# A new written order for all pieces of the first stage, and one layout for u's buffers

## The chip, the cores and the metric

The kernel runs on one core of a Trainium2 chip. The metric is device time in microseconds (us). The core has five engines, each with its own queue of instructions: TensorE (PE, with its weight loads as PEld), VectorE (DVE), ScalarE (ACT), GpSimd (POOL) and SyncE (SP), which issues the DMAs.

## The reference

The input `x` (2048 tokens, 512 channels, bf16) passes twice through a convolution layer A and an MLP layer B, each time as a residual:

```python
x = A_q
x = x + _A_ref(_layernorm(x), A_k, A_v, A_shift_k, A_ssm_k, A_ssm_D)
x = x + _B_ref(_layernorm(x), B_w1, B_b1, B_w2, B_b2)
x = x + _A_ref(_layernorm(x), A_k, A_v, A_shift_k, A_ssm_k, A_ssm_D)
x = x + _B_ref(_layernorm(x), B_w1, B_b1, B_w2, B_b2)
```

`_A_ref(q, k, v, ...)` shifts `k` by a four-tap filter for each channel, multiplies with `v` to u, convolves u along the 2048 tokens with `ssm_k` (a Fourier transform of length 4096, a product, a transform back), adds u times `ssm_D`, and multiplies with `q`. `_B_ref` is layer normalisation, a matmul to 1376 columns, gelu, and a matmul back to 512. k, v and the filters are the same in both A layers, so the convolution is computed once.

## The kernel before

The kernel has two stages. The first computes the convolution Y and the head of the first MLP; it runs to about 100 us. The second is a loop over eight groups of four token blocks (four groups, twice), each with two matmuls, `mm1` (L732) and `mm2` (L766), gelu on ACT and the normalisations on DVE.

The first stage is cut into some 340 pieces. A class `_Plan` collects them, each with a name and the code that it issues; `plan.write(ORDER)` then issues them in the order of a long string. A word of it is a name, a dot, the engine (P, A, D, G for POOL, S for SP) and digits for the buffers: a piece on PE names its slot of PSUM (`ps`, four of them) and, where it opens one, its buffer `xb` or `zt`. Each engine runs its own pieces strictly in this order, so a piece that waits holds all that stand behind it on its engine. A name with `e` at the end is the evacuation of the PE piece of that name, from PSUM to SBUF, on ACT or DVE (helper `evac`, L210 and L212), which frees the slot. The letters, with cc the quarter of the channels (0 to 3) and j the quarter of the 32 first-step frequencies:

- `lk`, `lv`, `lK`, `lW`, `lM`, `lx`, `w1`, `w2` and so on: loads. `kT`, `dg`, `kv`, `kvm`: the taps on PE and the product with v, for three quarters of the channels. `kg`, `ka`, `kgm`: taps, sums and the product with v of the last quarter, on POOL (L445, L452, L456), from which U3 starts.
- `KS`, `K2`: both steps of the filter's transform; `sa`, `sb`: eight copies of its result to a second layout (512 KB each).
- `U{cc}S{q}`: first step of u's transform, 4 matmuls into one PSUM slot, evacuated to a buffer `ZT` (L302). `U{cc}T{h}`: its 128x128 blocks transposed, 16 on PE for the quarters 0 to 2 (L334, evacuated at 128x2048), by DMA for quarter 3 (L281).
- `X{cc}{j}`: second step (L548), evacuated to an `xb` buffer. `T{cc}{j}`: the product of that buffer with the filter's spectrum, in SBUF, 128x2048 elements, on DVE or POOL (L563). T33 is cut into halves a and b. `V{cc}{j}`: first step of the transform back (L571), evacuated into a `ZT` buffer, or into the arena for quarter 0.
- `Z{cc}{g}`: transposes of V's results by DMA (L619) for the quarters 0 to 2, and `TD{g}` on PE (L607) for quarter 3; g is the token group. `Y{g}{t}`: last step (L639).
- `s00` to `s02`, `g`, `h`, `p`, `b`: normalisation, gate, statistics, power (POOL, L248) and normalisation again of the first token group; `LT`: its transposes (L647); `M`: the first MLP matmul (L695), which needs `w1`. Its gelu is L703.

The product of a T piece reads an `xb` buffer twice and two blocks of the spectrum, which it overwrites:

```python
kk = at(64 * K + 8 * K * cc + 2 * ka * CW, [[-32 * K, 2], [1, n * CW]])
x2 = apf(xb, xb.offset + (ka - k0) * CW, [list(xb.ap[0]), [0, 2], [1, n * CW]])
eng.tensor_tensor(kk, x2, kk, ALU.mult)
```

`w1` is loaded over the filter's spectrum of the first quarters, so it waits for V0 and V1, and for its place in SP's queue.

Of the kernel before, what the change touches and what calls it, by code (L numbers as in the profile page):

```python
# [103 lines left out]
def kernel(ctx: ExitStack, tc: tile.TileContext, A_q, A_k, A_v, A_shift_k, A_ssm_k, A_ssm_D,  # L104
                 B_x, B_w1, B_b1, B_w2, B_b2, out):
    nc = tc.nc
    P = 128
    _, S, D = A_q.shape
# [50 lines left out]
    IDt = const.tile([P, P], BF16, name="IDt")  # L159
# [23 lines left out]
    h = KS - 1  # L183
# [14 lines left out]
    ZTb = [big.tile([P, 8 * D], BF16, name=f"ZT{i}") for i in range(NZT)]  # L198
# [74 lines left out]
    with tc.tile_pool(name="ps", bufs=1, space=bass.MemoryType.PSUM) as ps:  # L273
# [10 lines left out]
        def mm_evac(name, ns, deps, mms, dims, dst, bf=False, take=(), free_mm=(), edeps=(), rank=0, src=None):  # L284
            src = src or (lambda v: v)
            n = int(np.prod(dims))
            cost = {"A": 85 + 0.82 * n, "D": 50 + (0.53 if bf else 1.06) * n}
            pe = plan.add(name, {"P": ns}, deps, lambda it: mms(view(pf[it["slot"]["ps"]], dims, BF16 if bf else None)),
                          take=["ps"] + list(take), free=free_mm, rank=rank)
            ev = plan.add(name + "e", cost, [pe] + list(edeps),  # L290
                          lambda it: evac(it["eng"], dst(), src(view(pf[pe["slot"]["ps"]], dims, BF16 if bf else None))),
                          free=[(pe, "ps")], rank=rank)
            return pe, ev

        def first_stage(name, src, cs, dst, deps, xbar, edeps):


            z, ze, sp = None, [], []
            for q in range(4):
                def mms(o, q=q):  # L300
                    for i in range(4):
                        nc.tensor.matmul(o[:, i, :], src[:, 4 * q + i, cs], Ft[:, 0:256], start=True, stop=True)  # L302
                hold = {}

                def zdst(q=q, hold=hold):
                    zt = ZTb[hold["pe"]["slot"]["zt"]]
                    if xbar:
                        return zt[:, :].rearrange("p (k j i) -> p k j i", k=NA, j=8)[:, :, :, 4 * q:4 * q + 4]
                    return zt[:, :].rearrange("p (j i k) -> p i j k", k=NA, j=8)[:, 4 * q:4 * q + 4, :, :]

                def zsrc1(v):
                    return v.rearrange("p i (j k) -> p k j i" if xbar else "p i (j k) -> p i j k", k=NA)
                pe, ev = mm_evac(f"{name}S{q}", 436, deps[q] + [z, lF], mms, [4, 2 * P], zdst,
                                 take=["zt"] if q == 0 else [], src=zsrc1)
                z = z or pe
                hold["pe"] = z
                ze.append(ev)
                sp.append(pe)
            first, out = [], []
            for h in range(2):  # L320
                def half(h=h):
                    return dst[:, 16 * h:16 * h + 16, :]
                if xbar:
                    t = turn(f"{name}T{h}", half, lambda h=h: ZTb[z["slot"]["zt"]][:, 2048 * h:2048 * h + 2048],
                             2 ** 19, ze + first + edeps, free=[(z, "zt")] if h == 1 else [])
                    out.append(t)
                    first = [t]
                    continue

                def mms(o, h=h):  # L330
                    for i in range(16):

                        zk = apf(ZTb[z["slot"]["zt"]], 16 * h + i, [[8 * D, P], [32, P]])
                        nc.tensor.transpose(o[:, i, :], zk, IDt[:])  # L334
# [15 lines left out]
        lF = load("lF", Ft[:], F_h.ap().bitcast(BF16), 2 ** 17)  # L350
# [16 lines left out]
        lW = load("lW", Wt[:], W_h.ap().bitcast(BF16), 2 ** 20)  # L367
        lH = load("lH", GPt[:], GP_h.ap().bitcast(BF16), 2 ** 16)
# [3 lines left out]
        for c in range(16):  # L372
            if c % (16 // NK) == 0:
                q = c * NK // 16
# [82 lines left out]
        kgm = plan.add("kgm", {"D": 1150, "G": 4200}, kg[-1:] + lv, gmul)  # L457
# [7 lines left out]
        lx0 = load("lx0", lna0, xd[:, 0:GT, :], 2 ** 19)  # L465
# [381 lines left out]
```

## Time and profile before

| | before |
|---|---|
| three timed runs, median | 248.03 us (246.64 to 249.02) |
| span of the profiled execution, first to last instruction | 245.9 us |
| the runs against that span | 0.8 to 3.1 us longer, 2.1 at the median, for what lies around it (the page lists no time of its own for the profiled execution) |
| `w1` issued, first matmul that reads it (L695) | 77.59 us, 85.62 us |
| first matmul of the second stage (L766) | 99.85 us |
| granted TensorE clock, mean | 0.998 |

In a line of the chain or the timeline, the numbers are the start and the length in us, then engine, line, operation and names; `<-` parts what is written from what is read, `x2` is a count, and brackets hold the idle time before and what ended it. In a line by group, the numbers behind the bar are busy us and the mean ns of one, then idle us. In a line by stretch, each engine has its busy us and its count.

### The profile page before, as it was taken

The page shows a single profiled execution, that of the slowest core. Times are in us where ns is not written, and L with a number is a line of the kernel's source. Part 1 is how long each engine was busy: PE and PEld are TensorE (multiplying, and loading weights), DVE is VectorE, ACT ScalarE, POOL GpSimd, SP SyncE. Part 2 cuts the span into 40 slices and gives each one's busy share as a digit, 9 for nine tenths or more (in the row PEclk, how much of TensorE's full clock was granted, in tenths as well). Part 3 has the DMA queues.
Part 4 walks back from the last instruction along what each step waited for, and adds up shares of the span by engine and source line. Part 5 has one row for each costly group of instructions (what it writes and reads, how often), then busy time and mean ns, then how long its engine had stood idle before and what let it go on. Part 6 is the DMA issues. An engine that isn't in the chain of part 4 may idle for free.

```text
span 245.9 us, 4897 instructions
## 1 busy us (share of the span) xinstructions
PE 236.2 (96%) x1989; PEld 142.5 (58%) x2002; DVE 169.9 (69%) x325; ACT 137.0 (56%) x197; POOL 62.5 (25%) x51
## 2 busy tenths in 40 slices
PE   6999999999997899999999999999999999999994
PEld 2898874898896588444444444444444444444443
DVE  0579799689998997878899898857956951021022
ACT  2706999989998989507307406506505604704700
POOL 2399999584000211111101111101011010000000
PEclk9999999999999999999999999999999999999999
DMA  6999907999999997040402104012025015011011
GB/s 248 346 259 185 287 16 248 356 387 223 306 173 183 255 159 235 3 87 0 85 0 53 36 0 85 3 35 51 1 58 115 0 43 128 3 43 43 0 42 43
DMA packets 56431, 29.64 MB, mean 121 GB/s; under 512 B 48883, under 2 KB 52696, under 8 KB 55514
## 3 DMA queue, kind: packets, MB, share of 16 engines
q1 hardware_dynamic: 56402, 29.34, 48.2%
q8 instruction: 15, 0.25, 0.4%
q14 instruction: 6, 0.05, 0.1%
q10 hardware_dynamic: 8, 0.00, 0.0%
HBM read 15.18 MB, written 2.10 MB: 70 GB/s over the span
## 4 chain that ended last, share of the span: by engine, by line
PE 81%; DVE 7%; ACT 3%; DMA 3%; issue 2%; SPq 1%; POOL 1%; DVEq 0%; POOLq 0%
PE po L766 31%; PE ph L732 27%; PE p L513 4%; PE p L695 4%; DVE arena L212 4%; DMA arena<-in_B_w_dram 3%; PE p L571 3%; PE p L412 2%; DVE arena L563 2%; PE p L334 2%; PE p L302 2%; ACT ZT L210 2%; PE p L384 1%; PE p L431 1%; PE p L548 1%
## 5 line engine op out<-in xcount | busy, mean ns | idle before, releaser
L734 ACT ACTIVATE arena<-ph,B 128x512 bf16<-128x512 f32 (+1 forms) x77 | 52.8, 687 | 79.1 <-PE ph L732 78.9
L766 PE MATMUL po<-arena 128*128 128x512 bf16 (+3 forms) x355 | 77.0, 372 | 0.4
L732 PE MATMUL ph<-arena 128*128 128x512 bf16 (+1 forms) x308 | 67.6, 379 | 0.0
L766 PEld LDWEIGHTS <-arena 128*128 128x128 bf16 (+1 forms) x363 | 35.5, 98 | 40.7
L771 DVE TENSOR_TENSOR arena<-po,arena 128x512 bf16<-128x512 f32 (+1 forms) x33 | 21.5, 672 | 44.5 <-PE po L766 44.5
L732 PEld LDWEIGHTS <-arena 128*128 128x128 bf16 (+1 forms) x308 | 30.8, 100 | 35.9
L210 ACT ACTIVATE arena<-p 128x1024 bf16<-128x1024 f32 (+6 forms) x43 | 38.8, 990 | 9.1 <-PE p L378 5.3
L248 POOL TENSOR_TENSOR lrsm<-lrsm,mhalf 128x4 f32<-128x4 f32 (+2 forms) x10 | 9.3, 927 | 78.8 <-DVE lrsm L242 78.8
L210 ACT ACTIVATE ZT<-p 128x1024 bf16<-128x1024 f32 (+1 forms) x22 | 21.0, 1006 | 0.9 <-PE p L302 0.4
L232 DVE BATCH_NORM_STATS2 lstm<-arena 128x6 f32<-128x512 bf16 x32 | 20.0, 681 | 0.2
L232 DVE BATCH_NORM_STATS2 lstg<-arena 128x6 f32<-128x512 bf16 x32 | 19.7, 678 | 0.0
L248 POOL TENSOR_TENSOR lrsg<-lrsg,mhalf 128x4 f32<-128x4 f32 x8 | 8.1, 1011 | 44.5 <-DVE lrsg L245 44.5
L563 DVE TENSOR_TENSOR arena<-xb,arena 128x2048 bf16<-128x2048 bf16 (+1 forms) x15 | 16.9, 1181 | 0.2 <-ACT xb L210 0.2
L571 PE MATMUL p<-arena 128*128 128x128 bf16 x256 | 16.2, 219 | 0.8 <-ACT xb L210 0.3
L253 DVE TENSOR_SCALAR arena<-arena,lmvg,lrsg 128x512 bf16<-128x512 bf16 x32 | 11.0, 409 | 7.9 <-POOL lrsg L248 7.9
L445 POOL TENSOR_TENSOR arena<-arena,SK 128x2048 bf16<-128x2048 bf16 (+3 forms) x4 | 14.9, 3750 | 3.6 <-ACT DG L423 3.4
L571 PEld LDWEIGHTS <-arena 128*128 128x128 bf16 x256 | 14.6, 98 | 2.1 <-DVE arena L563 1.2
L212 DVE CAST arena<-p 128x1024 bf16<-128x1024 f32 (+1 forms) x14 | 14.6, 1088 | 1.6 <-ACT arena L210 0.7
L210 ACT ACTIVATE xb<-p 128x1024 bf16<-128x1024 f32 x14 | 13.8, 1040 | 0.7 <-PE p L548 0.5
L253 DVE TENSOR_SCALAR arena<-arena,lmvm,lrsm 128x512 bf16<-128x512 bf16 x32 | 11.4, 413 | 2.2 <-POOL lrsm L248 2.2
L212 DVE COPY arena<-p 128x2048 bf16<-128x2048 bf16 (+3 forms) x10 | 10.2, 1025 | 3.5 <-PE p L334 1.4
L452 POOL TENSOR_TENSOR arena<-arena 128x2048 bf16<-128x2048 bf16 x3 | 12.2, 4066 | 0.2
(74 smaller groups left out, 231.5 us busy)
## 6 DMA issues: line engine op xcount, KB each, us to landing
arena<-arena SPq DMA_DIRECT2D x8, 512.0 KB, 8.7
arena<-in_A_k_dram SPq DMA_DIRECT2D x2, 1024.0 KB, 6.3
arena<-in_A_v_dram SPq DMA_DIRECT2D x2, 1024.0 KB
arena<-in_A_ssm_k_dram SPq DMA_DIRECT2D x4, 512.0 KB, 7.1
arena<-tabM SPq DMA_DIRECT2D x1, 2048.0 KB, 9.3
out_dram<-arena SPq DMA_DIRECT2D x15, 128.0 KB, 1.7
arena<-in_A_q_dram SPq DMA_DIRECT2D x1, 1536.0 KB, 6.8
arena<-in_B_w_dram SPq DMA_DIRECT2D x1, 1376.0 KB, 8.0
```

The lines of the kernel that those rows point to most:

```text
L210: nc.scalar.activation(dst, src, AF.Copy)
L212: nc.vector.tensor_copy(dst, src)
L232: nc.vector.bn_stats(self.st[:, i, 0, :], x_t[:, GT * g + i, :] if src is None else src[:, i, :])
L248: nc.gpsimd.tensor_tensor(self.rs[:, a:b], self.rs[:, a:b], mhalf[:, a:b], ALU.pow)
L253: nc.vector.tensor_scalar(out=dst[:, i, :], in0=xs, scalar1=self.mv[:, i, 0:1], scalar2=self.rs[:, i:i + 1], op0=ALU.subtract, op1=ALU.mult)
L445: nc.gpsimd.tensor_tensor(m[:, t:NT, :], kn[:, 0:NT - t, c3], sk(t, NT - t), ALU.mult)
L563: eng.tensor_tensor(kk, x2, kk, ALU.mult)
L571: nc.tensor.matmul(o[:, i, :], spec[:, cc, ka + i, :], Mt[:, ka + i, r, :], start=r == 0, stop=r == 1)
L732: nc.tensor.matmul(o.rearrange("p (i t) -> p i t", t=P), W1t[:, ct, ft * P:ft * P + m], lt[:, a:b, ct, :], start=ct == 0, stop=ct == CT - 1)
L734: nc.scalar.activation(hT[0:m, ft, a * P:b * P], o, AF.Gelu_apprx_tanh, bias=B1[0:m, ft:ft + 1])
L766: nc.tensor.matmul(po[:, a:b], hT[0:m, ft, i * P:(i + 1) * P], W2t[0:m, ft, a:b], start=ft == 0, stop=ft == FT - 1)
L771: nc.vector.tensor_tensor(xs, po[:, a:b], xs, ALU.add)
```

## The change

Two things. All pieces keep their work, but the string `ORDER` is written anew: their order, the engine of 45 of them, and the buffers. And the buffers between U's S and T pieces have one layout, (frequency, position, time block), for all four quarters. Before, only quarter 3 had it, and the quarters 0 to 2 had (position, time block, frequency), from which PE's transposes read every 32nd element.

```diff
 ORDER = """
-lk0.S lSK.S wm0.P0 bS.P2 bSK.P1 lk1.S bSe.A lb1.S kT1.P0 lF.S ...
+wm0.P0 lk0.S lSK.S bS.P3 bSe.D dg1.D lb1.S lh113.S lF.S lk1.S ...
 """
...
                 def zdst(q=q, hold=hold):
                     zt = ZTb[hold["pe"]["slot"]["zt"]]
-                    if xbar:
-                        return zt[:, :].rearrange("p (k j i) -> p k j i", k=NA, j=8)[:, :, :, 4 * q:4 * q + 4]
-                    return zt[:, :].rearrange("p (j i k) -> p i j k", k=NA, j=8)[:, 4 * q:4 * q + 4, :, :]
+                    return zt[:, :].rearrange("p (k j i) -> p k j i", k=NA, j=8)[:, :, :, 4 * q:4 * q + 4]
 
                 def zsrc1(v):
-                    return v.rearrange("p i (j k) -> p k j i" if xbar else "p i (j k) -> p i j k", k=NA)
+                    return v.rearrange("p i (j k) -> p k j i", k=NA)
...
                 def mms(o, h=h):
                     for i in range(16):
-
-                        zk = apf(ZTb[z["slot"]["zt"]], 16 * h + i, [[8 * D, P], [32, P]])
-                        nc.tensor.transpose(o[:, i, :], zk, IDt[:])
+                        nc.tensor.transpose(o[:, i, :], ZTb[z["slot"]["zt"]][:, (16 * h + i) * P:(16 * h + i + 1) * P], IDt[:])
```

The diff takes four lines out, so a line behind it has a number lower by two to four: the T product L563 is L559 in the changed kernel, the transposes L619 are L615, and `mm2` L766 is L762.

On POOL, around the end of the last quarter's taps, before has these rows (L452 is `ka3`, the five behind it are `s01` and `kgm`, then T00 from xb0 and T20 from xb2, then the first powers):

```order
L452 TENSOR_TENSOR arena_64<-arena_64 128x16x128
L245 TENSOR_SCALAR lrsg0_106<-lmvg0_105 128x4
L248 TENSOR_TENSOR lrsg0_106<-lrsg0_106,mhalf_77 128x4
L489 TENSOR_TENSOR am0_125<-lmvg0_105,lrsg0_106 128x4
L490 TENSOR_SCALAR am0_125<-am0_125 128x4
L456 TENSOR_TENSOR arena_64<-arena_64 128x16x128
L563 TENSOR_TENSOR arena_64<-xb0_95,arena_64 128x2x1024
L563 TENSOR_TENSOR arena_64<-xb2_97,arena_64 128x2x1024
L248 TENSOR_TENSOR lrsm0_112<-lrsm0_112,mhalf_77 128x1 x2
```

and the changed kernel these (`ka3`, `kgm`, then T10, T00, T01, T03, T21 and the two halves of T33):

```order
L448 TENSOR_TENSOR arena_64<-arena_64 128x16x128
L452 TENSOR_TENSOR arena_64<-arena_64 128x16x128
L559 TENSOR_TENSOR arena_64<-xb0_95,arena_64 128x2x1024
L559 TENSOR_TENSOR arena_64<-xb1_96,arena_64 128x2x1024
L559 TENSOR_TENSOR arena_64<-xb5_100,arena_64 128x2x1024
L559 TENSOR_TENSOR arena_64<-xb3_98,arena_64 128x2x1024
L559 TENSOR_TENSOR arena_64<-xb0_95,arena_64 128x2x1024
L559 TENSOR_TENSOR arena_64<-xb7_102,arena_64 128x2x512 x2
L248 TENSOR_TENSOR lrsm0_112<-lrsm0_112,mhalf_77 128x1 x2
```

`s01` has moved ahead of `kg3`, and five whole products and two halves stand where two whole ones stood.

On DVE, at the first T pieces, before has these rows (U2T1, two more U pieces, U1T0, U1T1, X22, then T23, T21, T01, T22, T03, T02):

```order
L212 COPY arena_64<-p3_122 128x16x128
L212 CAST ZT1_93<-p1_120 128x256x4
L212 COPY arena_64<-p2_121 128x16x128
L212 COPY arena_64<-p1_120 128x16x128
L212 CAST xb4_99<-p2_121 128x1024
L563 TENSOR_TENSOR arena_64<-xb0_95,arena_64 128x2x1024
L563 TENSOR_TENSOR arena_64<-xb5_100,arena_64 128x2x1024
L563 TENSOR_TENSOR arena_64<-xb1_96,arena_64 128x2x1024
L563 TENSOR_TENSOR arena_64<-xb4_99,arena_64 128x2x1024
L563 TENSOR_TENSOR arena_64<-xb6_101,arena_64 128x2x1024
L563 TENSOR_TENSOR arena_64<-xb2_97,arena_64 128x2x1024
```

and the changed kernel these (T12, the evacuation of U2T0, T13, T11, X20, T02, V13, X23, T20, X30, T23, T22; behind them stand T30, T31, V22, T32, V31):

```order
L559 TENSOR_TENSOR arena_64<-xb2_97,arena_64 128x2x1024
L212 COPY arena_64<-p3_122 128x16x128
L559 TENSOR_TENSOR arena_64<-xb6_101,arena_64 128x2x1024
L559 TENSOR_TENSOR arena_64<-xb4_99,arena_64 128x2x1024
L212 CAST xb8_103<-p0_119 128x1024
L559 TENSOR_TENSOR arena_64<-xb7_102,arena_64 128x2x1024
L212 CAST ZT2_94<-p1_120 128x32x32
L212 CAST xb2_97<-p2_121 128x1024
L559 TENSOR_TENSOR arena_64<-xb8_103,arena_64 128x2x1024
L212 CAST xb4_99<-p2_121 128x1024
L559 TENSOR_TENSOR arena_64<-xb2_97,arena_64 128x2x1024
L559 TENSOR_TENSOR arena_64<-xb1_96,arena_64 128x2x1024
```

Before, the products on DVE stand nearly in one block, behind U's evacuations; now products and evacuations alternate.

On SP, around `w1`, before has these rows (U3T0, `lx`, U3T1, `ly`, then Z21 Z20, Z00 Z01, Z22, Z10 Z11, `w1`):

```order
L281 DMA_TRANSPOSE arena_64<-ZT1_93 128x16x128
L278 DMA arena_64<-in_A_q_dram 128x2048
L281 DMA_TRANSPOSE arena_64<-ZT1_93 128x16x128
L278 DMA arena_64<-in_A_q_dram 128x6144
L619 DMA_TRANSPOSE arena_64<-ZT0_92 128x8x128 x2
L619 DMA_TRANSPOSE arena_64<-arena_64 128x8x128 x2
L619 DMA_TRANSPOSE arena_64<-ZT0_92 128x8x128
L619 DMA_TRANSPOSE arena_64<-ZT1_93 128x8x128 x2
L278 DMA arena_64<-in_B_w1_dram 128x4x1376
```

and the changed kernel these (U3T0, `ly`, U3T1, `lx`, then Z11 Z10 Z13, Z03 Z00, Z20 Z23, `w1`):

```order
L281 DMA_TRANSPOSE arena_64<-ZT0_92 128x16x128
L278 DMA arena_64<-in_A_q_dram 128x6144
L281 DMA_TRANSPOSE arena_64<-ZT0_92 128x16x128
L278 DMA arena_64<-in_A_q_dram 128x2048
L615 DMA_TRANSPOSE arena_64<-ZT2_94 128x8x128 x3
L615 DMA_TRANSPOSE arena_64<-arena_64 128x8x128 x2
L615 DMA_TRANSPOSE arena_64<-ZT1_93 128x8x128 x2
L278 DMA arena_64<-in_B_w1_dram 128x4x1376
```

Seven transposes stand ahead of `w1` in both; the last two were of quarter 1 (Z10, Z11), and are of quarter 2 now (Z20, Z23).

More of the change, by code (lines that the diff above doesn't have):

```diff
@@ new lines @@
+wm0.P0 lk0.S lSK.S bS.P3 bSe.D dg1.D lb1.S lh113.S lF.S lk1.S kT0.P1 bB.P2 bBe.D lh1.S dg0.D kT1.P0 lv0.S kT1e.D kT0e.A kT3.P3 bSK.P2 kT2.P1 lK10.S bSKe.A kv01.P0 kg0.G kg1.G kT3e.D kT2e.D dg2.A kvm01.D kv00.P2 lH.S lK00.S kv20.P3 kd4.P1 kvm00.D kd4e.D U1S0.P00 lx0.S lv1.S kvm20.D KS51.P2 U1S0e.A lK11.S KS41.P1 KS51e.A U2S0.P31 lK01.S KS50.P0 KS41e.D KS50e.A KS40.P2 kv03.P1 KS40e.A kd0.P0 U2S0e.D kv21.P3 s00.D kvm03.D U0S0.P22 kd0e.A U0S0e.A kv02.P0 kvm21.D KS10.P2 KS00.P1 kvm02.D KS10e.A KS01.P3 kd6.P0 KS11.P2 KS00e.A kd6e.D KS61.P0 U1S3.P1 KS01e.D KS71.P3 ka1.G KS61e.D KS11e.A kg2.G U1S3e.A KS60.P2 KS71e.D kd2.P0 U1S1.P1 kd2e.A U1S1e.D U0S3.P0 KS30.P3 KS60e.A lW.S lM.S ka2.G KS31.P2 KS30e.D U0S3e.A KS31e.A KS21.P1 KS20.P0 KS70.P3 KS20e.D U0S1.P2 KS21e.A U0S1e.D U2S1.P1 U1S2.P0 KS70e.A K23.P3 U2S1e.A K20.P2 K23e.D K27.P1 U1S2e.A K22.P0 K20e.A K21.P3 K25.P2 K27e.D K21e.D K22e.A K26.P1 s01.G K24.P0 K215.P3 K25e.A K26e.D K24e.A U0S2.P2 K213.P1 kg3.G K215e.D U0S2e.A K213e.A K211.P0 K214.P2 K212.P3 K211e.D K212e.D K214e.A K28.P1 U1T0.P0 ka3.G K29.P2 kgm.G K28e.A sa0.S K210.P3 U1T1.P1 U1T0e.D K29e.A K210e.A U2S2.P2 U2S2e.A U1T1e.D U3S0.P00 s02.D U0T0.P3 X10.P10 sb0.S sa1.S U3S2.P2 U3S0e.A U0T1.P0 X10e.A sb1.S sa3.S U0T0e.D U0T1e.D U3S2e.A U3S1.P1 X00.P31 U3S3.P2 X00e.D U3S1e.A T10.G U3S3e.A X12.P02 sb2.S X12e.A U2S3.P1 X03.P33 U2S3e.D X11.P24 X01.P05 X03e.A X01e.A sb3.S X13.P16 T00.G U2T0.P3 X13e.A sa2.S X02.P07 X11e.D U2T1.P2 T12.D U2T0e.D X02e.A V10.P12 X20.P08 T13.D U2T1e.A V12.P3 V10e.A V00.P2 V13.P1 V12e.A T11.D V00e.A U3T0.S X20e.D T02.D ly.S X21.P00 V11.P3 U3T1.S lx.S V13e.D X21e.A V11e.A Z11.S X23.P22 X22.P01 T01.G X31.P16 X23e.D Z10.S T03.G V02.P3 X22e.A X31e.A X30.P24 V02e.A T20.D X30e.D V01.P0 T23.D T21.G V01e.A X33.P17 T22.D X32.P35 V03.P2 T30.D X33e.A V03e.A X32e.A T31.D V20.P01 V22.P1 V22e.D V23.P2 V21.P3 Z13.S T32.D V20e.A V30.P00 Z03.S T33a.G Z00.S V23e.A V31.P2 V21e.A V30e.A Z20.S Z23.S w1.S T33b.G V31e.D V32.P1 V33a.P3 Z01.S Z21.S V33b.P0 V32e.A V33be.A wm2.P2 wm1.P1 V33ae.D TD0a.P2 TD0b.P3 Z12.S TD0ae.D Y00.P1 TD0be.D Y00e.A TD3.P0 TD3e.A Y01.P2 Y02.P3 TD2.P0 g00.D w4.S h00.D Z02.S p00.G Y30.P1 Y01e.A Y02e.A Y32.P3 g01.D TD2e.A TD1.P0 b00.D h01.D p01.G g02.D LT0.P2 b01.D Y30e.A LT0e.A M0a.P1 h02.D LT1.P2 Y32e.A Z22.S M0b.P3 LT1e.D TD1e.A M0ae.A p02.G M0be.A Y10.P0 Y10e.A M1a.P2 b02.D LG1.D LT2.P1 Y12.P3 LT2e.A M1b.P0 M1ae.A w2.S Y12e.D M2b.P1 Y20.P3 M1be.A M2c.P2 M2a.P0 M2be.A M2ce.A Y22.P1 Y20e.A w3.S M2ae.A Y22e.A
```

1 line of the change is left out of this document (removed).

## The prediction

> **What bounds the kernel now.** I read the engine totals first, then the chain that ended last, then busy times by stretch.
>
> ```profile
> PE 236.2 (96%) x1989; PEld 142.5 (58%) x2002; DVE 169.9 (69%) x325; ACT 137.0 (56%) x197; POOL 62.5 (25%) x51
> ...
> 77.59 7.99 DMA arena<-in_B_w_dram
> ...
> 85.62 2.64 PE p L695 x44
> ...
> 99.85 8.43 PE po L766 x39
> ```
>
> The first row says that TensorE (PE) bounds the whole, but that is an average over two stages. In the chain, the second matmul of the MLP (L766) starts at 99.85 us and runs on PE alone to the end; the change touches nothing there, so those 146 us stand. What it can move is the time until then. There the chain passes through the load of `w1`, issued at 77.59 and landed 7.99 us later, and the first L695 matmul starts at 85.62. Before that load:
>
> ```profile
> core 0: us, PE busy (x) PEld busy (x) DVE busy (x) ACT busy (x) POOL busy (x), PEclk, DMA share, GB/s
> 48.00:58.00 10.00, 9.86 (x147) 9.32 (x146) 8.74 (x8) 8.88 (x10) 8.15 (x2) 1.00 1.10 337
> 58.00:77.00 19.00, 18.20 (x305) 16.93 (x301) 18.79 (x18) 18.93 (x22) 0.00 (x1) 1.00 1.09 234
> ```
>
> From 58 to 77 us VectorE (DVE) and ScalarE (ACT) are both full, 18.79 and 18.93 of 19 us, and GpSimd (POOL) does nothing. This is the stretch of the spectral products (the T pieces, L563) and of the matmuls behind them (V). Work taken off DVE here should pay, if it can truly run beside DVE.
>
> **What the change moves.** Of the 17 T pieces, before gives 15 to DVE and two to POOL; after gives ten to DVE and seven to POOL (T10, T00, T01, T03, T21, and the halves T33a and T33b). The evacuations are dealt out anew between ACT and DVE.
>
> ```profile
> L563 DVE TENSOR_TENSOR arena<-xb,arena 128x2048 bf16<-128x2048 bf16 x13 | 15.6, 1257 | 0.0
> L563 POOL TENSOR_TENSOR arena<-xb,arena 128x2048 bf16<-128x2048 bf16 x2 | 8.1, 4090 | 3.2 <-DMA arena<-arena 3.2
> L210 ACT ACTIVATE ZT<-p 128x1024 bf16<-128x1024 f32 x20 | 20.0, 1041 | 0.9 <-PE p L302 0.4
> L212 DVE CAST ZT<-p 128x1024 bf16<-128x1024 f32 x7 | 8.5, 1216 | 0.1
> ```
>
> A whole T takes 1.26 us on DVE and 4.09 us on POOL, so POOL gets 5 x 4.09 + 2 x 2.05 (the halves, an estimate) = 24.6 us. DVE loses five whole T and two halves and gains T20; it takes 17 evacuations of 1024 columns from ACT and gives 12 back. Summed with these rows, DVE's work up to the last T stays near 62 us and ACT's falls from about 60 to 56. The balance looks fair: ten T on DVE beside 24.6 us of POOL. It rests on the two running side by side.
>
> **What they do side by side.** Before has one place where a T on DVE meets a T on POOL.
>
> ```profile
> 49.85 8.15 POOL L563 TENSOR_TENSOR arena<-xb,arena 128x2048 bf16<-128x2048 bf16 x2 [3.18 <-DMA arena<-arena]
> ...
> 53.59 1.22 DVE L212 COPY arena<-p 128x2048 bf16<-128x2048 bf16 x1 [0.46 <-PE p L334]
> 54.99 1.23 DVE L212 COPY arena<-p 128x2048 bf16<-128x2048 bf16 x1 [0.18 <-PE p L334]
> ...
> 57.26 1.82 DVE L563 TENSOR_TENSOR arena<-xb,arena 128x2048 bf16<-128x2048 bf16 x1
> ...
> 59.01 1.21 DVE L563 TENSOR_TENSOR arena<-xb,arena 128x2048 bf16<-128x2048 bf16 x1
> ```
>
> POOL's two products end at 49.85 + 8.15 = 58.00. The copies out of PSUM at 53.59 and 54.99 lie wholly beside them and take their usual 1.22. The first T on DVE starts at 57.26, with all its waits over, and ends at 59.08: 1.82 us long where the next takes 1.21, and 1.08 after POOL's end. So it did nothing until POOL had finished. Had the two shared at half speed, 0.74 us of overlap would have cost 0.37, not 0.61. POOL waits for DVE too:
>
> ```profile
> 82.44 0.58 POOL L248 TENSOR_TENSOR lrsm<-lrsm,mhalf 128x1 f32<-128x1 f32 x1 [24.44 <-DVE lrsm L242]
> 84.83 0.94 POOL L248 TENSOR_TENSOR lrsm<-lrsm,mhalf 128x1 f32<-128x1 f32 x1 [1.80 <-DVE lrsm L242]
> ...
> 84.67 0.68 DVE L666 TENSOR_TENSOR arena<-arena 128x1024 bf16<-128x1024 bf16 x1
> ```
>
> The same one-column power takes 0.58 us at 82.44 and 0.94 at 84.83, where DVE multiplies two SBUF operands until 85.35; from there to its end are 0.42 us. I take it that a product of two SBUF operands on DVE and one on POOL exclude each other, and that whoever comes second waits for the whole of the first.
>
> The Trainium skill states this as a rule (SBUF — State Buffer, "Who interferes with whom"): a DVE instruction with two SBUF inputs contends with a GpSimd instruction that reads SBUF, and the later one blocks until the earlier is through. The trace agrees with it, by 1.82 against 1.21 us.
>
> Before meets this once; after puts six of POOL's seven products among DVE's ten.
>
> **The walk through the T stretch.** POOL's work ahead of its first T is the same in both orders (the four taps, the sums, one normalisation, `kgm`):
>
> ```profile
> 42.56 4.11 POOL L456 TENSOR_TENSOR arena<-arena 128x2048 bf16<-128x2048 bf16 x1
> ```
>
> It ends at 46.67. After lets U3S0, U0T0 and X10 follow on PE (0.45 + 1.0 + 0.5 us) and the evacuation of X10 on ACT (1.0), so T10 starts at about 49.9 on POOL, where T00 does now. POOL then holds T10 until 54.0 and T00 until 58.1. DVE has as much work ahead of its first T (T12) as before had ahead of T23, 41 us by the rows, and reaches it between 54.5 and 57.3. Either way it waits until 58.1. From there, with 1.15 us from start to start for a T or an evacuation on DVE (the rows 57.26 and 59.01 belong to a run of seven in 8.64; six of them take 6.89), a DVE piece that waits going first when POOL ends, and POOL's next when that one ends:
>
> - T12 58.1 to 59.25, then U2T0's evacuation to 60.4; POOL has T01 59.25 to 63.35, so T13 runs 63.35 to 64.5.
> - T03 on POOL to 68.6; T11 waits for it, 68.6 to 69.75; X20's evacuation to 70.9.
> - T21 on POOL needs X21, whose PSUM slot that evacuation frees; 0.5 on PE and 1.0 on ACT later it is 72.4. Meanwhile T02 runs freely to 72.05, V13 to 73.2, X23 to 74.35.
> - T21 72.4 to 76.5; T20 waits, to 77.65; X30 to 78.8.
> - T33a comes ready at about 78.0 and T33b behind it. T23 waits until 80.05, T22 until 83.25.
> - T22, T30, T31 end at 86.7, V22's evacuation at 87.85, T32 at 89.0.
>
> Six waits: 3.1 + 2.95 + 4.1 + 2.15 + 1.25 + 2.05 = 15.6 us. Behind T32 stand V32, V33a and V33b on PE (0.9 + 0.9) and an evacuation (0.7), so the transposes of the last quarter (TD0) start at 91.6.
>
> ```profile
> 73.33 4.09 SPq L619 DMA_TRANSPOSE arena<-ZT  x3
> 77.59 0.46 SPq L278 DMA_DIRECT2D arena<-in_B_w_dram  x1
> ...
> 78.02 0.71 PE L607 MATMUL p<-IDt,ZT 128*128 128x128 bf16 x8 [0.87 <-ACT ZT L210]
> ...
> 83.80 0.40 PE L647 MATMUL p<-IDt,arena 128*128 128x128 bf16 x4 [0.21 <-DVE arena L253]
> ```
>
> TD0 starts at 78.02 now, so it is 13.6 late. For `w1`: SyncE (SP) works its queue in order, and after places two transposes of V2's results (Z20, Z23) just ahead of `w1`. They need V22's evacuation, 87.85; with 1.36 us each (4.09 for three), `w1` issues at 90.5 instead of 77.59 and lands at 98.5. The other way to the first L695 matmul goes from TD0 over the gate and the normalisations to LT0 (78.02 to 83.80) and its evacuation (1.0): 98.4. The two meet, and PE starts the MLP at 98.5 instead of 85.62: **12.9 us later**. Behind it stand the same pieces as before (seven M, two LT, four of the Y), 14.2 us from 85.62 to 99.85, and then the unchanged 146.
>
> Sum: the profiled execution spans 245.9 us; with 12.9 that is 258.8. The runs have a median of 248.03, 2.1 above that span for what lies around it; 248.03 + 12.9 = **260.9**.
>
> **The parts that I cost at little.** The new layout: buffers of u between its stages are written by the evacuation in runs of four, and read by PE in rows of 128.
>
> ```profile
> 33.50 1.22 DVE L212 CAST ZT<-p 128x1024 bf16<-128x1024 f32 x1
> ...
> 51.91 1.22 DVE L212 CAST ZT<-p 128x1024 bf16<-128x1024 f32 x1
> ...
> 44.17 1.03 PE p L334 x16
> ...
> 7.74 1.45 PE p L431 x24
> ```
>
> The evacuation at 33.50 (U1S2) writes the old layout, the one at 51.91 (U3S1) the layout that all get: 1.22 both, so writing costs nothing. Reading: 16 strided transposes take 1.03, 64 ns each; 24 from rows (L431) take 1.45, 60 ns each. Six groups of 16 gain 96 x 4 ns = 0.4 us, at 44 to 55 us, where PE waits for slots that DVE and ACT have yet to free; I count nothing. U2T1's evacuation moves to ACT at twice 1024 columns, at most 2 x 1.04 us; ACT has the 4 us that it gained. One DVE normalisation (s02, 1.37) moves ahead of the stretch, where `kgm` has just ended; if DVE comes early, it waits for that at most a few tenths. `lM` is issued earlier than 37.67 and the eight copies behind it land before 57.7; that would let V start sooner, but the T pieces are later than the copies in any case.
>
> If PE's waits in this stretch (up to 5 us by the walk) drop its clock, PE gets slower behind them; the granted clock is 1.00 in both stretches above, so no row here has that price. The Trainium skill (TensorE: Matmul & The Clock Gate, "What's actually happening") halves the clock after an idle window of about 3.4 us; by it the V pieces behind two such waits would cost an estimated 1 to 2 us more, making 262 to 263.
>
> **Rivals.**
> - *No blocking: T23's 0.61 us had another cause.* Then DVE runs its 16 pieces from T12 (55.0) to T32 in 18.4 us, to 73.4, and POOL ends T33b at 49.9 + 24.6 = 74.5. V33b's evacuation ends near 76, TD0 starts 2.0 us earlier than 78.02, `w1` about as much: 246.0, on the other side. It decides if POOL's products cost DVE's less than 2 us in all. Against it stand the two rows that were slower exactly beside the other engine.
> - *A collision costs what it did, no more.* Six to ten collisions at 0.61 make 3.7 to 6.1 us, less the 2.0: 249.7 to 252.1, say 251.5. For it: that is the only price measured. Against: DVE's end followed POOL's end within the time of its own work.
> - *The ties fall otherwise.* If POOL's next product goes ahead of a waiting DVE, T12 waits past T01 and T03 too (to 66.8) but the later ones less: about 1.2 more, 262. If DVE keeps the right of way while T pieces follow one another, T11 and T23, T22 wait less: about 3 us less, 258. Both belong to the likeliest case.
> - *The layout as the whole gain*, with the order neutral: 0.4 us, 247.6. The order rows show POOL's queue to differ, so it can't be neutral unless the first rival holds.
>
> **Numbers.** Full blocking 0.70, with its own range 257 to 263.5; cheap collisions 0.14; no blocking, with or without the layout's gain, 0.13; later trouble that I don't see 0.03. The range takes in the first two: 250.5 to 264. A measurement of this kernel tells about 1% (2.5 us) from no change. Faster by over 1% needs more than the 2.0 of the first rival: 0.05. Within 1%: the rest of it and a little of the second: 0.12. Slower: 0.83.
>
> **What the next profile would show.** Full blocking: L559 on DVE (T) x10 with a mean near (10 x 1.21 + 15.6) / 10 = 2.8 us instead of 1.26, single ones of 3 to 5 us that end 1.1 after a POOL product; `w1` issued near 90.5; the first L762 matmul near 112.7, and the same distance from it to the end as now. Wrong if those means stay near 1.25, or if DVE reaches T12 only after 58, when POOL would have passed some of its products alone.

## The result, and the profile after

The changed kernel takes **262.44 us** (median of 5 runs, 261.98 to 263.14). Before, run beside it on the same chip, takes 248.03 (5 runs, 246.64 to 249.02). The ratio is 1.059, with a 95% interval of 1.057 to 1.062: 14.4 us slower. The forecast was 260.9, in a range of 250.5 to 264.

The profiled execution of the changed kernel has a span of 261.4 us, 15.5 more than the 245.9 of before. Its own run took 263.14, the longest of the five, 0.7 above their median. The totals by engine, first row of its page:

```profile
PE 240.0 (92%) x1989; PEld 146.9 (56%) x2002; DVE 185.4 (71%) x328; ACT 132.1 (51%) x189; POOL 82.1 (31%) x56
```

DVE's busy time rose by 15.5 us (169.9 before), although it has ten products where it had 13 and two halves. That is the loss, seen on the engine that was meant to be relieved. The chain that ended last shows where it enters:

```profile
89.55 1.14 DVE ZT L212
90.69 1.14 DVE arena L559
...
92.98 1.52 ACT ZT L210 x2
...
94.55 0.71 PE p L603 x8
...
101.14 0.61 ACT arena L210
...
101.78 1.95 PE p L691 x32
...
115.78 3.24 PE po L762 x15
```

The chain no longer passes through the load of `w1`. It comes from the last product on DVE (T32, L559 at 90.69) by two evacuations on ACT to TD0 (L603) at 94.55, where before had 78.02: 16.5 us late. The MLP's first matmul starts at 101.78 (85.62 before, 16.2 late), the second stage at 115.78 (99.85, 15.9 late). From there to the end nothing changed. The products by group, and then in order of time, first DVE's and then POOL's:

```profile
L559 DVE TENSOR_TENSOR arena<-xb,arena 128x2048 bf16<-128x2048 bf16 x10 | 26.0, 2633 | 0.5 <-ACT xb L210 0.5
L559 POOL TENSOR_TENSOR arena<-xb,arena 128x2048 bf16<-128x2048 bf16 x5 | 22.1, 4452 | 7.9 <-ACT xb L210 7.9
```

```profile
57.84 3.67 DVE L559 TENSOR_TENSOR arena<-xb,arena 128x2048 bf16<-128x2048 bf16 x1 [0.49 <-ACT xb L210]
...
62.57 8.93 DVE L559 TENSOR_TENSOR arena<-xb,arena 128x2048 bf16<-128x2048 bf16 x2
...
72.56 1.21 DVE L559 TENSOR_TENSOR arena<-xb,arena 128x2048 bf16<-128x2048 bf16 x1
...
77.49 2.53 DVE L559 TENSOR_TENSOR arena<-xb,arena 128x2048 bf16<-128x2048 bf16 x1
...
81.09 8.47 DVE L559 TENSOR_TENSOR arena<-xb,arena 128x2048 bf16<-128x2048 bf16 x4
...
90.61 1.21 DVE L559 TENSOR_TENSOR arena<-xb,arena 128x2048 bf16<-128x2048 bf16 x1
```

```profile
52.34 18.08 POOL L559 TENSOR_TENSOR arena<-xb,arena 128x2048 bf16<-128x2048 bf16 x4 [3.46 <-ACT xb L210]
74.89 4.06 POOL L559 TENSOR_TENSOR arena<-xb,arena 128x2048 bf16<-128x2048 bf16 x1 [4.47 <-ACT xb L210]
81.81 5.53 POOL L559 TENSOR_TENSOR arena<-xb,arena 128x1024 bf16<-128x1024 bf16 x2 [2.86 <-ACT xb L210]
```

A product on DVE takes 2633 ns in the mean instead of 1257. Where POOL has nothing (T02 at 72.56, T32 at 90.61) it takes 1.21 as ever. T12 starts at 57.84 and ends at 61.51; T13 and T11, behind one evacuation, take 8.93 together. POOL's second product ends at 60.43, and T12 ends 1.08 later. POOL waits in its turn: its third and fourth product take 5.03 each instead of 4.07.

One product of each, cut out of the same two views, shows a turn:

```profile
66.43 5.07 DVE L559 TENSOR_TENSOR arena<-xb,arena 128x2048 bf16<-128x2048 bf16 x1
```

```profile
65.39 5.03 POOL L559 TENSOR_TENSOR arena<-xb,arena 128x2048 bf16<-128x2048 bf16 x1
```

T11 on DVE begins at 66.43, stands until T03 on POOL ends at 70.42, and is through 1.08 later. T03 began at 65.39 but had itself stood until T13 was through on DVE at 66.51. While two engines stand so, the others do as well:

```profile
core 0: us, PE busy (x) PEld busy (x) DVE busy (x) ACT busy (x) POOL busy (x), PEclk, DMA share, GB/s
58.00:77.00 19.00, 11.48 (x140) 11.18 (x138) 17.55 (x8) 8.37 (x8) 14.53 (x4) 0.73 0.54 154
```

In the stretch from 58 to 77 us, where ACT had 18.93 busy us of 19 and PE 18.20, ACT now has 8.37 and PE 11.48. DVE is "busy" for 17.55 us with 8 instructions, where before it did 18.

### The profile page after: what moved, and what is told of

It reads as the page before. It is cut to its first block, busy times and chain, and to the rows that moved or that the text cites. A ratio compares the mean times of both kernels' runs of the same rounds, so it can differ in the third digit from the quotient of the medians.

```text
span 261.4 us, 4901 instructions
## 1 busy us (share of the span) xinstructions
PE 240.0 (92%) x1989; PEld 146.9 (56%) x2002; DVE 185.4 (71%) x328; ACT 132.1 (51%) x189; POOL 82.1 (31%) x56
## 4 chain that ended last, share of the span: by engine, by line
PE 62%; DVE 1%; ACT 1%; issue 0%
PE po L762 29%; PE ph L728 25%; PE p L691 4%; PE p L635 3%; PE p L603 1%; ACT ZT L210 1%; DVE arena L559 0%; DVE ZT L212 0%; PE p L567 0%; PE p L643 0%; ACT arena L210 0%; DVE arena L767 0%
## 5 line engine op out<-in xcount | busy, mean ns | idle before, releaser
L762 PE MATMUL po<-arena 128*128 128x512 bf16 (+3 forms) x355 | 77.0, 372 | 0.4
L762 PEld LDWEIGHTS <-arena 128*128 128x128 bf16 (+1 forms) x363 | 35.5, 98 | 40.7
L210 ACT ACTIVATE arena<-p 128x1024 bf16<-128x1024 f32 (+6 forms) x40 | 37.5, 1004 | 10.0 <-PE p L427 4.4
L559 POOL TENSOR_TENSOR arena<-xb,arena 128x2048 bf16<-128x2048 bf16 (+1 forms) x7 | 27.7, 3975 | 10.8 <-ACT xb L210 10.8
L559 DVE TENSOR_TENSOR arena<-xb,arena 128x2048 bf16<-128x2048 bf16 x10 | 26.0, 2633 | 0.5 <-ACT xb L210 0.5
L567 PE MATMUL p<-arena 128*128 128x128 bf16 x256 | 18.3, 235 | 4.4 <-DVE arena L559 3.5
L567 PEld LDWEIGHTS <-arena 128*128 128x128 bf16 x256 | 17.0, 107 | 5.2 <-DVE arena L559 4.4
L232 DVE BATCH_NORM_STATS2 lstg<-arena 128x6 f32<-128x512 bf16 x32 | 19.7, 678 | 0.0
L212 DVE CAST arena<-p 128x1024 bf16<-128x1024 f32 (+1 forms) x16 | 16.9, 1106 | 1.3 <-PE p L374 0.9
L544 PE MATMUL p<-arena,Wt 128*128 128x128 bf16 x128 | 10.2, 236 | 7.6 <-DVE xb L212 5.0
L210 ACT ACTIVATE xb<-p 128x1024 bf16<-128x1024 f32 x11 | 10.9, 1078 | 6.5 <-DVE arena L559 5.9
L544 PEld LDWEIGHTS <-Wt 128*128 128x128 bf16 x128 | 8.9, 106 | 8.4 <-issue 5.6
```

The lines of the kernel that those rows point to most:

```text
L210: nc.scalar.activation(dst, src, AF.Copy)
L212: nc.vector.tensor_copy(dst, src)
L232: nc.vector.bn_stats(self.st[:, i, 0, :], x_t[:, GT * g + i, :] if src is None else src[:, i, :])
L544: nc.tensor.matmul(o[:, i, :], Wt[:, k0 + i, :], chunk(ZX, cc)[:, k0 + i, :], start=True, stop=True)
L567: nc.tensor.matmul(o[:, i, :], spec[:, cc, ka + i, :], Mt[:, ka + i, r, :], start=r == 0, stop=r == 1)
L762: nc.tensor.matmul(po[:, a:b], hT[0:m, ft, i * P:(i + 1) * P], W2t[0:m, ft, a:b], start=ft == 0, stop=ft == FT - 1)
```

## Experiments

The theory is the prediction's: a product of two SBUF operands on DVE and one on POOL exclude each other, each waits for the whole of the other, and the waits make the loss. The rivals: POOL's help is real and the order of the rest is at fault; or the new layout costs.

**The two engines by themselves.** A kernel that leaves the whole convolution and MLP out, and runs products on POOL beside one kind of DVE or ACT work at a time, with a meeting point (`gate`) between the pairs; it ran once. `gp(2)` is two products of 128x2048 on POOL, `dve("two", 6)` six of the same on DVE; each has other buffers than its neighbour, so no data ties the two together. An excerpt:

```diff
+        gate()
+        gp(2)
+        gate()
+        dve("two", 6)
+        for kind, n, g in (("two", 6, 3), ("psum", 6, 2), ("copy", 6, 2), ("stats", 9, 2), ("scal", 9, 2)):
+            gate()
+            gp(g)
+            dve(kind, n)
```

> Computes nothing of the reference: it writes the input back and measures pairs of engines. Each stretch starts two or three POOL products of 128x2048 in bf16 and, some 0.4 us later, a run of one kind on VectorE: products of two SBUF operands, products of a PSUM and an SBUF operand, copies from PSUM, statistics, and subtract-and-multiply by columns, all but the first half as long or shorter; at the end copies on ScalarE beside POOL. Exclusion of SBUF products: the first kind takes turns with POOL (1.2 and then 4 to 5 us, POOL 5 instead of 4.1 us), those with PSUM, the copies, the statistics and ScalarE keep their lengths and POOL its 4.1. Sharing by bandwidth instead: all VectorE products beside POOL become longer by the same share, and no single one waits 3 us or more.

By DVE's timeline and then POOL's (L56 and L69 are the products of two SBUF operands, L58 a product with one operand in PSUM, L60 a copy out of PSUM, L62 statistics of one SBUF tensor, L64 the normalisation's subtraction and product with one SBUF tensor):

```profile
16.77 7.52 DVE L56 TENSOR_TENSOR do<-a,a 128x2048 bf16<-128x2048 bf16 x6 [7.22 <-ACT a L50]
25.05 18.70 DVE L56 TENSOR_TENSOR do<-a,a 128x2048 bf16<-128x2048 bf16 x6 [0.76 <-ACT a L50]
44.56 7.52 DVE L58 TENSOR_TENSOR do<-f,a 128x1024 bf16<-128x1024 f32 x6 [0.81 <-ACT f L51]
53.37 7.52 DVE L60 CAST do<-f 128x1024 bf16<-128x1024 f32 x6 [1.29 <-ACT f L51]
62.10 6.52 DVE L62 BATCH_NORM_STATS2 st<-a 128x6 f32<-128x512 bf16 x9 [1.21 <-ACT a L50]
70.89 11.48 DVE L64 TENSOR_SCALAR do<-a,st 128x512 bf16<-128x512 bf16 x9 [2.27 <-ACT a L50]
```

```profile
8.00 8.17 POOL L69 TENSOR_TENSOR po<-b,b 128x2048 bf16<-128x2048 bf16 x2 [1.98 <-ACT a L50]
25.06 15.08 POOL L69 TENSOR_TENSOR po<-b,b 128x2048 bf16<-128x2048 bf16 x3 [8.90 <-ACT f L51]
```

Alone, six DVE products take 7.52 us and two on POOL 8.17, so three would take 12.2. Side by side, six and three take 18.70 together: 7.5 + 12.2 = 19.7 is the sum of the two, and the missing 1.0 is what neighbours overlap by at the changes of turn. No product runs beside another. In order, DVE's six take 1.23, 4.95, 4.95, 4.95, 1.23, 1.23: one of each in turn, whoever waits goes next. Three DVE products are slowed by 3.7 us each, and POOL's by about 1. Beside products with an operand in PSUM, copies from PSUM, statistics, and copies on ACT, POOL kept its 8.17 to 8.19 us for two, and none of these instructions was longer there than it is in the kernel before where POOL stands idle (a copy 1.22 us here and 1.21 there at 65.82, a statistic 0.69 here and there at 81.26).

**Only T10 stays on POOL.** In the changed kernel, T00, T01, T03, T21, T33a and T33b go to DVE at the same places in the order (here and below, only the changed words of `ORDER` are shown).

```diff
-T00.G  T01.G  T03.G  T21.G  T33a.G  T33b.G
+T00.D  T01.D  T03.D  T21.D  T33a.D  T33b.D
```

> The changed kernel with T00, T01, T03, T21 and both halves of T33 given back to VectorE at the same places of the order; POOL keeps T10 alone, which ends before VectorE reaches its first T. VectorE gets 5.8 us more work. Exclusion of the two engines' products: no T waits any more (all near 1.21 us), T32 ends near 80.4 instead of 91.8, and the time falls by about 11 to 251 (250 to 253). New order at fault in some other way, POOL's help being real: VectorE's 5.8 us come on top, 268, and not below 262. TensorE's lower clock at fault: no change beyond 2 us unless its waits vanish too.

252.20 us (251.84 to 252.54), 1.017 times before, interval 1.015 to 1.019. The group of DVE's products and its chain:

```profile
L559 DVE TENSOR_TENSOR arena<-xb,arena 128x2048 bf16<-128x2048 bf16 x14 | 16.7, 1226 | 0.0
```

```profile
82.85 0.71 PE p L603 x8
...
90.25 1.95 PE p L691 x32
```

DVE does four whole products and two halves more (6.3 us by 1.22 and 0.69) and is through earlier, TD0 at 82.85 instead of 94.55. Taking these six pieces away from POOL, some 20 us of its work, makes the kernel 10.2 us faster. That settles the main question against "POOL's help is real". TD0 is still 4.8 us later than before (78.02), and the time 4.3 us longer. By the two orders, DVE has one product and eight evacuations more here than before, which points at its work; that this is the whole of it isn't shown.

**Two fewer on POOL.** The same for T01 and T03 alone, the two for which T13 and T11 stood.

```diff
-T01.G  T03.G
+T01.D  T03.D
```

> The changed kernel with T01 and T03 given back to VectorE, the other five products left on POOL. Exclusion: the waits of T13 and T11 (2.7 and 3.9 us) go, 2.3 us of work come, so about 4.3 us less, 258. Order at fault, POOL's help real: 2.3 more, 264.7.

258.53 us (257.85 to 259.41), 1.043 times before, interval 1.039 to 1.046; as the theory had it. The mean of a product on DVE falls to 1866 ns:

```profile
L559 DVE TENSOR_TENSOR arena<-xb,arena 128x2048 bf16<-128x2048 bf16 x12 | 22.0, 1866 | 0.4 <-DMA arena<-arena 0.4
```

**One product to POOL in the kernel before.** The other direction, in the order of before: T02 goes from DVE to POOL.

```diff
-T02.D
+T02.G
```

> The kernel before with one word changed: T02 on POOL instead of VectorE, in the middle of VectorE's run of T pieces. Exclusion: POOL gets in between two of VectorE's products and holds the next one for about 4.1 us; VectorE is spared 1.15; the time grows by about 3 to 251. No exclusion: VectorE is spared 1.15 and the time is 247 to 248.

251.92 us (251.56 to 253.77), 1.017 times before, interval 1.013 to 1.021. DVE is relieved of 1.21 us and the kernel is 3.9 us slower than before was beside it (247.92). Its trace is of the longest of its runs. From it the timelines of POOL, DVE and PE:

```profile
61.99 4.17 POOL L563 TENSOR_TENSOR arena<-xb,arena 128x2048 bf16<-128x2048 bf16 x1 [3.10 <-ACT xb L210]
```

```profile
58.04 11.47 DVE L563 TENSOR_TENSOR arena<-xb,arena 128x2048 bf16<-128x2048 bf16 x6
72.70 1.23 DVE L212 CAST ZT<-p 128x1024 bf16<-128x1024 f32 x1 [3.19 <-PE p L571]
```

```profile
67.30 7.14 PE L571 MATMUL p<-arena 128*128 128x128 bf16 x80 [4.24 <-DVE arena L563]
```

The same place before:

```profile
57.26 8.64 DVE L563 TENSOR_TENSOR arena<-xb,arena 128x2048 bf16<-128x2048 bf16 x7
65.82 1.21 DVE L212 CAST ZT<-p 128x1024 bf16<-128x1024 f32 x1
```

Six products take 2.83 us longer than seven did: T22 stood for T02. Behind that, PE stood 4.24 us for T22 and then took 7.14 us for 80 matmuls, 89 ns each in the mean; the same 80 took 4.88 before (62.55 on PE), 61 each. DVE waited 3.19 us for them where before it waited none. So a collision costs the wait, and up to as much again behind it when PE comes back slow. The granted clock there is 0.79 from 60 to 70 us and 0.87 from 70 to 80, against 1.00 before.

**The layout alone, and the order alone.** Before's `ORDER` with the changed code, and the changed `ORDER` with before's code.

```diff
 (the changed kernel)
-ORDER = """wm0.P0 lk0.S lSK.S bS.P3 ..."""
+ORDER = """lk0.S lSK.S wm0.P0 bS.P2 ..."""
```

> The old order with the one layout. Strided reads gone, 0.4 us less at most: 247.5 to 248.0 beside 247.9. If writing in runs of four costs the evacuations something, above 248.5.

> The new order with the two old layouts. The layout gives PE 96 x 4 ns = 0.4 us where it waits for VectorE anyway: 262.4, between 261.5 and 263.5. If the layout had a part in the loss, the time falls by that part; if it hides a gain, the time is above 263.5.

Layout alone: 248.15 us (247.03 to 249.14, 12 runs), ratio 1.001, interval 0.998 to 1.004. Order alone: 263.82 (262.87 to 264.97), ratio 1.064, interval 1.059 to 1.069. The loss is the order's. Order alone lies 1.4 us above the changed kernel and just above 263.5, the sign named for a hidden gain of the layout; with four runs that overlap those of the changed kernel (261.98 to 263.14), whether the layout is worth something in the new order stays open. The strided weight loads did cost PE something, 150 ns against 98 (PE's weight loads of U's transposes, before and with the layout alone), but in a place where PE waits for others:

```profile
L334 PEld LDWEIGHTS <-ZT 128*128 128x128 bf16 x96 | 6.8, 150 | 0.2
```

```profile
L330 PEld LDWEIGHTS <-ZT 128*128 128x128 bf16 x96 | 5.7, 98 | 0.4
```

**The early loads.** In the trace after, POOL's taps (`kg0`) start at 13.31 instead of 11.11, and `kgm` ends at 48.88 instead of 46.67, so T10 starts at 52.34 where the walk had 49.9. The second half of k (`lk1`) had moved from third to sixth place among the first loads. This run gives the loads before's order.

```diff
-lk0.S lSK.S ... lb1.S lh113.S lF.S lk1.S ... lh1.S
+lk0.S lSK.S ... lk1.S lb1.S lF.S lh1.S lh113.S
```

> The changed kernel with the first seven loads in the order of before, the second half of k third instead of sixth. If the late start of POOL's taps (13.3 us instead of 11.1) sets the start of the T stretch, all of it moves forward by 2.2 to 2.4 us: 260.1. If VectorE's collisions hide it, 262.4.

262.65 us (261.77 to 263.09), ratio 1.060, interval 1.056 to 1.064: no difference from the changed kernel's 262.44. By its time it is the second of the two cases named, but not for the reason named there: it isn't that collisions hid an earlier start; T10's start itself moved by 0.95 us only (51.39), within what it varies by. POOL's timeline:

```profile
11.91 7.97 POOL L441 TENSOR_TENSOR arena<-arena,SK 128x2048 bf16<-128x2048 bf16 x2 [4.42 <-ACT SK L210]
...
51.39 13.09 POOL L559 TENSOR_TENSOR arena<-xb,arena 128x2048 bf16<-128x2048 bf16 x3 [3.91 <-ACT xb L210]
```

The profiles of all kernels here tell why. The start of `kg0` differs from execution to execution: 11.11, 11.42 and 11.89 in the three with before's whole order, 11.79 to 13.31 in the four with the changed order and its loads, 11.22 to 11.91 in the four with the changed order and the early loads. The 13.31 was the latest of them; the loads explain perhaps 1 us of it. T10 starts 3.4 to 3.9 us behind the end of `kgm` with the changed order and early loads, and T00 2.7 to 3.3 behind it with before's order, so about half a microsecond more lies between `kgm` and the first product. Nor is `kgm` always what T10 waits for. With the new order alone, `kgm` ended at 47.33, but PE came to U3S0 only at 51.06, without a gap behind its other pieces, and T10 started at 54.25:

```profile
54.25 8.13 POOL L563 TENSOR_TENSOR arena<-xb,arena 128x2048 bf16<-128x2048 bf16 x2 [6.93 <-ACT xb L210]
```

How the rest splits is not settled.

**Towards a better version.** T10 alone on POOL, the early loads, and three evacuations (X11, X23, V22) moved from DVE to ACT, which stood idle. Three places for `w1` in SP's queue: ahead of the transposes Z03, Z00, Z20, Z23 (`best`), between Z00 and Z20 (`best3`), and behind all four as in the changed kernel (`best2`).

```diff
-X11e.D ... X23e.D ... V22e.D
+X11e.A ... X23e.A ... V22e.A
```

> The changed kernel with those early loads, POOL left with T10 alone, three evacuations of the T stretch (X11, X23, V22) moved from VectorE to ScalarE, and w1 issued right behind Z13 instead of three transposes of quarter 2 later. No product waits; VectorE's T32 ends near 74 and TD0 starts near 77, one us before the old kernel; w1 no longer sets the end, the way through the gate does. 246.5, between 245 and 249. If POOL's help were real, taking six products from it would leave it above 255.

> The changed kernel with before's order of the first seven loads, all T pieces but T10 on DVE, and three evacuations (X11, X23, V22) moved from DVE to ACT; w1 stays behind Z23 as in the changed kernel. If w1 ahead of the Z transposes was what the run with w1 moved forward lost, T32 ends near 76 and TD0 starts near 80.3 as there, LT0's way (6.8 us by before) ends near 87.1, w1 is issued near 78.1 and lands near 86.1, so the MLP starts near 87.1: 1.5 us later than before, 249.5 us. If the transposes were late for another reason, the MLP starts near 89.2 again and the time is 252 to 253. Full exclusion has no part in the difference, since no T piece on DVE has one on GpSimd beside it but T00.

> The same kernel with w1 between Z00 and Z20 in SyncE's queue. w1 is issued near 75 and lands near 83 to 85; Z00 lands ahead of it, but Z20 and Z23 now share the DMA engines with it. If a transpose behind w1 takes up to 7.5 us to land, Z20 lands near 84 and the first Y waits for it: MLP near 88 to 90, 250.5 to 252.5. If the transposes don't suffer, LT0's way (87.1) is last: 249.5, no better than with w1 behind Z23, since the load isn't what comes last there.

| `w1` | time, us | ratio to before | TD0, us | first MLP matmul in the chain, us |
|---|---|---|---|---|
| ahead of the four | 253.05 (251.04 to 253.89) | 1.021 (1.017 to 1.025) | 80.29 | 89.23 |
| between | 254.86 (254.37 to 255.00) | 1.028 (1.025 to 1.031) | 80.16 | 93.07 |
| behind them | 250.28 (249.97 to 250.38) | 1.009 (1.006 to 1.013) | 80.04 | 88.53 |

The first was to give 246.5 and missed: TD0 came 3.3 us later than the 77 it counted on, of which the 2.2 to 2.4 us that the early loads were to give and didn't are probably the most; the rest lies behind TD0. Its trace is of its fastest run (251.04, granted clock 1.000); the other five had 0.986 to 0.993 and took 1.4 to 2.9 us more, so the table's points are better than its median. The chain of the one with `w1` ahead, at that place:

```profile
74.73 7.53 DMA arena<-arena
82.26 0.85 issue
83.11 0.59 PE p L635 x2
```

and with `w1` behind:

```profile
80.04 0.73 PE p L603 x8
...
88.53 1.95 PE p L691 x32
```

A transpose issued behind `w1` took 7.53 us to land, and the first Y (L635) waited for it until 83.11. With `w1` behind them, Z20 took 4.9 (from 77.38) and Y came at 82.41, with a time between the two cases named (249.5, and 252 to 253), nearer the first. So `w1` ahead of the transposes only exchanged one wait for another. With `w1` between, the loss was larger than either expectation (254.86 against at most 252.5). Z20, now behind it, held Y up until 84.37, 2.4 us later by its evacuation (85.41 against 83.04). PE had then run no matmul for 3.49 us, and its clock was halved. The stretches of that run:

```profile
82.00:84.00 2.00, 0.00 (x0) 0.00 (x0) 0.00 (x0) 0.00 (x0) 0.00 (x0) 0.82 0.60 83
...
86.00:88.00 2.00, 2.00 (x8) 0.76 (x6) 1.81 (x3) 1.52 (x3) 0.00 (x0) 0.50 1.01 190
88.00:90.00 2.00, 2.00 (x12) 1.30 (x11) 1.92 (x6) 1.17 (x2) 0.59 (x1) 0.50 0.81 157
```

The transposes TD3 and TD2, eight each, took 1.06 us instead of 0.66 there, the six Y matmuls between them 2.76 instead of 1.46. Together that is the other 2.1 of the 4.5 us between the two at the MLP's start. The expectation had left the clock out. None of the three beats before.

## Why the prediction was right

**The mechanism** held. Products of two SBUF operands on DVE and POOL run in series, seen in four kernels and in the pair by itself. Of the rivals, "no blocking" (246.0) and "a collision costs what it did" (251.5) are out: a product that is stopped stands for up to 3.9 us (T11), not 0.61. The 0.61 in the trace of before was the tail of a collision, because DVE came when POOL had 0.74 us left. The Trainium skill (SBUF — State Buffer, "Who interferes with whom") has a DVE instruction with two SBUF inputs contend with a GpSimd one that reads SBUF, by an exclusive lock that blocks the other fully; these runs agree, by 4.95 us against 1.23.

**The walk.** Six waits were forecast, and six came:

| | T12 | T13 | T11 | T20 | next | next | sum, us |
|---|---|---|---|---|---|---|---|
| forecast | 3.1 | 2.95 | 4.1 | 2.15 | T23 1.25 | T22 2.05 | 15.6 |
| measured, less 1.21 | 2.46 | 2.73 | 3.86 | 1.32 | T22 1.93 | T30 1.93 | 14.2 |

Turns were taken as assumed, DVE first when POOL ends and POOL next. T33a came at 81.81, later than the walk's 78.0, so the last two waits fell on T22 and T30 and T23 ran free. From T12's release to TD0 the walk had 33.5 us (58.1 to 91.6), and 34.1 were measured (60.43 to 94.55). That they are so close is in part luck: the five waits behind the release came to 0.7 us less than forecast, and DVE stood 1.45 us ahead of X23's evacuation, which the walk didn't have.

One reading ahead of the walk was wrong: DVE loses four whole products (T10, T01, T03, T21) and two halves, not five and two, and gains T20, from 13 to ten. The sum of DVE's work that it went into is off by one product (1.2 us); the walk, which goes piece by piece, doesn't use it.

**The step that was off** is "POOL's work ahead of its first T is the same in both orders, so T10 starts at about 49.9". The work is the same, its start isn't: T10 began at 52.34 in the profiled execution (50.7 to 54.3 in the four profiles with the changed order and loads), T00 before at 49.66 to 50.76 in three. DVE reached T12 at 57.84, behind the forecast 54.5 to 57.3 but still ahead of POOL's end, so only T10's start counts. All later points shift with it:

| | forecast, us | measured, us |
|---|---|---|
| POOL's second product ends | 58.1 | 60.43 |
| T32 ends | 89.0 | 91.82 |
| TD0 starts | 91.6 | 94.55 |
| `w1` issued | 90.5 | 93.48 |
| MLP starts | 98.5 | 101.78 |
| second stage starts | 112.7 | 115.78 |

The sum said +12.9. Between the two traces it is +16.2 at the MLP's start: 2.3 more at POOL's second product, 0.6 in the stretch and 0.3 behind TD0. By the medians it is +14.4: the profiled execution was the longest of its kernel, 0.7 above the median, and by the end of the trace the +16.2 had shrunk to 15.5. With T10's start ranging over 3.6 us in the four profiles, a median within 1.6 us of the forecast is partly luck. The two ways to the MLP met as forecast: `w1` landed at about 101.4, the first transposes (LT0) were evacuated at 101.74.

**The clock** fell, which the sum had left out and a sentence beside it had priced at 1 to 2 us. The changed kernel by two-microsecond stretches:

```profile
58.00:60.00 2.00, 2.00 (x40) 2.00 (x37) 2.00 (x1) 2.00 (x3) 2.00 (x1) 1.00 1.23 228
60.00:62.00 2.00, 0.20 (x4) 0.03 (x1) 2.00 (x2) 2.00 (x2) 2.00 (x2) 1.00 0.76 301
...
64.00:66.00 2.00, 2.00 (x22) 2.00 (x20) 2.00 (x1) 0.74 (x1) 2.00 (x2) 0.50 1.12 241
...
74.00:76.00 2.00, 2.00 (x22) 2.00 (x20) 0.90 (x1) 1.37 (x2) 1.11 (x1) 0.50 0.00 0
```

After PE stood from 60.21 to 62.70 the clock was 0.50, and again after it stood from 67.66 to 72.69; V11's 16 matmuls took 1.91 us behind the second stop (73.50), where 16 at full clock took 1.06 (59.15). Most of it lies beside DVE's waits. DVE itself waited 1.45 us ahead of X23's evacuation at 76.35, with PE at half clock just before, which agrees with that price at its lower end. The halving is as the Trainium skill states it (TensorE: Matmul & The Clock Gate, "What's actually happening"). Its idle window of about 3.4 us was not needed in full: here 2.50 us without a matmul went with the drop.

**The layout** was rightly costed at nothing in before's order: 248.15 against 247.82, with an interval across 1. In the new order that stays open (263.82 without it).

## What to carry to other kernels

Before work is dealt from DVE to GpSimd, look at what both read. Two products of SBUF operands didn't overlap in any trace here, and each one of this size (128x2048, bf16) that was moved beside others cost about four microseconds of the pair's time for the 1.2 that DVE saves; put on GpSimd what runs beside DVE's reads from PSUM, or in a stretch where DVE has nothing of the kind. A rise of an instruction's mean time (1257 to 2633 ns at one shape) is the sign, since the wait is counted as busy time. And a single short collision in a trace shows only what was left of the other instruction, not its price.

## What was not expected of the hardware

The subtraction and product with one SBUF tensor (L64 of the pair kernel) is also held up beside POOL. Nine take 11.48 us: 4.21, 4.08, then 0.41 each once POOL had ended. POOL kept its 8.17 for two. The first is recorded as starting 0.02 us ahead of POOL's product (70.89 and 70.91) and stood for it all the same. The Trainium skill (SBUF — State Buffer, "Who interferes with whom") does say that `tensor_scalar` can enter the modes that take the shared port pair; I had counted only two-operand products. In this kernel the normalisations of the first stage are of that kind. None of them stood for a T piece on POOL in the trace after: the one in that stretch (s02) ran from 50.11 to 51.48, when POOL was idle, and the next at 100.24.

In the pair kernel the turns went strictly one for one. While POOL had a queue of products, no two short DVE products ran in a row, nor did POOL get two in a row while DVE waited, which is why 3.7 us were lost each time.
